# Rounding turns in the matmul accumulator: one TensorE step for one VectorE step, a norm moved to ScalarE, and new instruction orders

## The chip, the cores and the metric

The kernel runs on one NeuronCore of a Trainium2 chip. Five engines work side by side: TensorE (PE in the profile, with its weight loads as PEld), VectorE (DVE), ScalarE (ACT), GpSimd (POOL) and SyncE (SP), which here only issues DMAs. Each takes its own instructions in a fixed order and waits at the head of its queue for what the instruction needs. The metric is the device time of one execution in microseconds (us), lower is better.

## The reference

Four layers are applied to a 2048x512 array, each after a layer norm and with a residual: a two-dimensional Fourier filter (A), a long convolution along the rows (B), then A and B once more with the same parameters.

```
def _A_ref(x, w_r, w_i):
    X = rfft2(x) * (w_r + 1j * w_i)
    return irfft2(X)
def _B_ref(u, log_A_real, A_imag, C_real, C_imag, log_dt, D_skip):
    dt = exp(log_dt); A = -exp(log_A_real) + 1j * A_imag
    P = exp((A * dt[:, None])[:, :, None] * arange(L))         # D x N x L
    K = 2 * einsum("dn,dnl->dl", (C_real + 1j * C_imag) * dt[:, None], P).real
    return irfft(rfft(u_t, 2L) * rfft(K, 2L))[:L] + u * D_skip
x = x + _A_ref(_layernorm(x));  x = x + _B_ref(_layernorm(x))
x = x + _A_ref(_layernorm(x));  x = x + _B_ref(_layernorm(x))
```

K, the kernel of the convolution, needs the cosine and sine of a phase for every channel, state and position. Its sum over 128 states for 512 channels and 2048 positions is a large part of the work, and both B layers use the one K.

## The kernel before

All transforms are matmuls with constant tables. Almost every matmul is issued in two halves of 64 output rows (`halves`, lines 325 to 330), so that the two column halves of the array work at once: this is the tile shape 128x64. The rows transform of a B layer (`rows` in `forward_b`, through `side_by_side`, lines 333 to 336) has 64 rows of contraction and uses the shape 64x64, four products at once. A change from one shape to the other is called a change of tile shape below.

The program has these stages: the start (loads, first layer norm, the small vectors that K is made of, `kernel_parts`), the first layer A (`layer_a`), the first layer B (`forward_norm`, `forward_b`, `layer_b`), the second layer A, the second layer B. Making K (`kernel_time`) runs beside the first two layers, because it needs nothing from them; its frequency form (`kernel_freq`) is needed block by block by the first layer B.

`kernel_time` works through 32 units. For each, `grow` makes three magnitudes by Exp on ScalarE, one of them by a product on GpSimd. `bend` then makes phases for each of two halves of a unit, 64 times in all. A phase is counted in turns (whole circles), so only its fraction matters. Two pairs of bf16 matmuls put the turns into a PSUM tile `pk` of 512 columns, 256 each (`KQ`, `KP`); VectorE adds and subtracts 1.5x2^23, which rounds to a whole number, and writes it as bf16 into the SBUF tile `kw` (line 864); a third pair of matmuls with minus the identity (`ni`) subtracts it from the turns in PSUM. On ScalarE `sine` takes the absolute value and the sine, `cosine` takes the sine with a quarter turn added. `terms` on VectorE (lines 886 and 888) multiplies them with the magnitudes, `total` sums over states on TensorE into `pv` (line 899), and ScalarE copies that out (line 907). The `pk` tiles rotate over three PSUM banks.

In the first layer B, `forward_norm` loads four row groups of the normed array by a DMA into a tile `w`, and applies the layer norm with a scale and a bias per partition from `norms`. `XNE` names the engine of each of the four: 'gggg' is GpSimd (line 1113), 64 instructions of 128x128 in all. These tiles are the weights' side of the 64x64 matmuls.

The order of the work on every engine is written out. `take_turns` numbers an engine's instructions as the code makes them and chains them in the order of the table `TURNS`; no instruction passes another on its engine. `ROOMS` says which buffer of a rotating tag each new tile takes. `WARM` (used in `ps`, line 312) puts throwaway matmuls on the tile `warm` ahead of the first use of some PSUM tiles: each count is one pair of halves, which keeps TensorE's activity up.

## Time and profile before

| | before |
|---|---|
| times of three runs | 716.46 us median (710.45, 716.46, 718.14) |
| span of the profiled execution, first to last instruction | 713.4 us |
| busy: TensorE, VectorE, ScalarE, GpSimd | 626.0, 601.9, 438.2, 357.3 us |
| mean granted TensorE clock, share of full speed | 0.973 |
| rows of matmuls on `warm` | 924 of 9580, 73.8 us busy |
| ACT table loads | 24 |

The profiled execution's own time is shown only as its span; the median of the runs is 3.1 us above that span. A matmul's row in the profile lasts from its start to its modelled end, which lies after the time at which the next one can start, so rows of TensorE overlap and its busy time is more than the time for which it is taken. A float32 matmul makes two rows, a bf16 one makes one.

### The profile page before, as it was taken

How to read it: one execution, taken by the hardware profiler on the slowest of the kernel's cores; microseconds unless marked ns; L12 is line 12 of the kernel's file. 1: busy time of each engine (PE TensorE's matmuls, PEld its weight loads, DVE VectorE, ACT ScalarE, POOL GpSimd, SP SyncE). 2: the span in 40 equal slices, each digit the busy share in tenths (PEclk: the TensorE clock that was granted, in tenths of full speed). 3: DMA queues.
4: the chain of work that ended last, by engine and by line, in shares of the span. 5: the costliest groups of instructions: out<-in, count | busy, mean ns of one | idle time of the engine just before them, and what ended most of it. 6: DMA issues, size and time to landing. Idle time of an engine off the chain costs nothing. (4 is left out here: it accounts for less than half of the span.)

```text
span 713.4 us, 23503 instructions
## 1 busy us (share of the span) xinstructions
PE 626.0 (88%) x9580; PEld 491.3 (69%) x9580; DVE 601.9 (84%) x1348; ACT 438.2 (61%) x946; POOL 357.3 (50%) x565
## 2 busy tenths in 40 slices
PE   4459989989996999889999997984989899999996
PEld 3237867878674867667858876774877766577876
DVE  4998497998999799969999676869588699799993
ACT  3558999997664796778868524333767427333322
POOL 1533528672852704543196356452056484286870
PEclk9779999999999999999999999997999999999999
DMA  8602611613558350455544689222123103335514
GB/s 282 229 0 89 210 48 47 122 62 43 167 133 245 107 138 32 65 128 94 163 62 136 195 198 246 80 106 75 61 77 89 46 2 104 125 103 149 156 34 111
DMA packets 137355, 81.32 MB, mean 114 GB/s; under 512 B 70976, under 2 KB 116928, under 8 KB 136352
## 3 DMA queue, kind: packets, MB, share of 16 engines
q1 hardware_dynamic: 136992, 79.30, 40.1%
q8 instruction: 76, 1.25, 0.7%
q0 software_dynamic: 256, 0.52, 0.4%
q14 instruction: 31, 0.25, 0.1%
HBM read 54.90 MB, written 25.43 MB: 113 GB/s over the span
## 5 line engine op out<-in xcount | busy, mean ns | idle before, releaser
L1003 POOL TENSOR_TENSOR u<-wb,wb 64x512 f32<-64x512 f32 x90 | 123.2, 1373 | 66.0 <-DVE wb L991 60.9
L336 PE MATMUL p<-z,mb 128*64 128x512 f32 (+2 forms) x480 | 108.0, 517 | 1.7 <-DVE wb L991 1.3
L899 PE MATMUL pv<-qp 128*64 128x128 f32 x1024 | 81.6, 279 | 5.0 <-ACT stage L907 4.2
L991 DVE TENSOR_TENSOR wb<-p,kk 128x512 f32<-128x512 f32 x128 | 81.5, 676 | 4.3 <-POOL u L1003 2.3
L336 PEld LDWEIGHTS p<-mb,u 128*64 128x64 f32 x2048 | 73.1, 138 | 13.1 <-issue 6.7
L336 PE MATMUL p<-mb,u 128*64 128x64 f32 x2048 | 74.3, 223 | 4.4 <-issue 2.0
L663 ACT COPY z<-p 128x512 f32<-128x512 f32 x96 | 52.4, 595 | 41.8 <-PE p L336 31.6
L669 DVE STREAM_TRANSPOSE z<-z 128x512 f32<-128x512 f32 x96 | 59.3, 675 | 19.8 <-ACT z L663 19.7
L899 PEld LDWEIGHTS pv<-qp 128*64 128x64 f32 x1024 | 64.4, 139 | 15.8 <-ACT stage L907 6.9
L1113 POOL TENSOR_SCALAR w<-w,norms 128x128 f32<-128x128 f32 x64 | 34.7, 554 | 67.7 <-DMA w<-h 29.8
L547 POOL TENSOR_TENSOR w<-w,w 64x257 f32<-64x257 f32 x48 | 34.7, 724 | 66.8 <-DVE w L542 45.3
L1015 ACT COPY u<-p 128x512 f32<-128x512 f32 x64 | 35.9, 590 | 48.7 <-PE p L336 45.3
L330 PE MATMUL p<-w,w 128*64 128x256 f32 x256 | 38.2, 438 | 27.8 <-DVE w L463 11.6
L330 PE MATMUL pk<-kb,th 96*64 96x256 bf16 (+1 forms) x384 | 56.5, 312 | 1.5 <-DVE qp L888 1.1
L542 DVE TENSOR_TENSOR w<-wt,p 128x514 f32<-128x514 f32 x64 | 42.7, 688 | 17.1 <-PE p L336 9.6
L864 DVE TENSOR_SCALAR kw<-pk 128x512 bf16<-128x512 f32 x64 | 42.9, 680 | 16.5 <-PE pk L330 16.1
L330 PE MATMUL p<-warm 128*64 128x128 f32 x612 | 49.2, 284 | 3.2 <-DVE half L1139 1.1
L336 PE MATMUL p<-t,w 64*64 64x128 f32 x1024 | 42.1, 280 | 10.2 <-DMA w<-kt 3.5
L336 PEld LDWEIGHTS p<-z,mb 128*64 128x64 f32 x480 | 39.7, 137 | 16.1 <-issue 7.9
L330 PEld LDWEIGHTS p<-w,w 128*64 128x64 f32 x256 | 24.7, 156 | 36.3 <-DVE w L463 12.7
L336 PE MATMUL p<-w,ca 128*64 128x257 f32 x256 | 45.0, 385 | 4.1 <-ACT w L526 1.5
L832 ACT ACTIVATE kf<-pk 128x512 f32<-128x512 f32 x64 | 38.8, 606 | 15.4 <-PE pk L330 13.8
(179 smaller groups left out, 1617.1 us busy)
## 6 DMA issues: line engine op xcount, KB each, us to landing
wt<-in_w SPq DMA_DIRECT2D x32, 257.0 KB, 2.7
kf<-kk SPq DMA_DIRECT2D x32, 256.0 KB, 3.3
kk<-kf SPq DMA_DIRECT2D x32, 256.0 KB, 2.7
u<-in_x SPq DMA_DIRECT2D x16, 256.0 KB, 6.8
hr<-in_x SPq DMA_DIRECT2D x16, 256.0 KB, 3.9
kt<-stage SPq DMA_DIRECT2D x32, 128.0 KB, 5.2
h<-hr SPq DMA_DIRECT2D x16, 256.0 KB, 3.0
w<-kt SPq DMA_DIRECT2D x32, 128.0 KB, 3.1
```

Of the source, the lines that this page charges most:

```text
L330: self.nc.tensor.matmul(out[64 * r:64 * r + 64], weights[:, 64 * r:64 * r + 64], data, **k)
L336: last = self.nc.tensor.matmul(out, weights, data, start=not more, stop=True, skip_group_check=True).ins
L542: nc.vector.tensor_mul(m[pl], W, px[:, None, :].to_broadcast([128, 2, 257]))
L547: e[0].tensor_sub(Y[0:64, v], m[0][hs, 0], m[1][hs, 1])
L663: nc.scalar.copy(tiles["z"][:, :, :, b, m:m + 2].rearrange("p u j m r -> p (u j) (m r)"), ps[b].rearrange("p u j m r -> p (u j) (m r)"))
L669: nc.vector.transpose(tiles["zt"][:, u:u + 8].rearrange("p u j d -> p (u j d)"), tiles["z"][:, u:u + 8].rearrange("p u j b m r -> p (u j b ...
L832: nc.scalar.activation(*a, **k)
L864: nc.vector.tensor_scalar(whole, p, MAGIC, -MAGIC, op0=ALU.add, op1=ALU.add)
L899: nc.tensor.matmul(p[64 * t:64 * t + 64, g], QP[:, c, 2, d:d + 2].rearrange("p s a -> p (s a)"), QP[:, c, 0:2, d:d + 2].rearrange("p k s b ...
L991: nc.vector.tensor_mul(split(m[c, pl], "du", [32, 16]), by_channel(p), split(k[c], "du", [32, 16]))
L1003: self.added = e[0].tensor_sub(y[0:64], v[0, 0], v[1, 1]), e[1].tensor_add(y[64:128], v[0, 1], v[1, 0])
L1015: nc.scalar.copy(V[:, :, j, :, d:d + 8].rearrange("p n q d -> p q n d"), p.rearrange("p (q n) d -> p q n d", q=2))
```

## The change

Five things change.

1. `bend` no longer uses VectorE. After the two pairs of products, two more pairs of matmuls add 1.5x2^23 to the PSUM tile and subtract it again: weights `ni`, now a row of ones or of minus ones in the first of 128 partitions, and a new tile `big` that holds the constant. The accumulation in PSUM rounds. Two last pairs with negated tables (`LQ`, `LP`) subtract the turns, so the tile holds the whole number minus the turns, and the sine's scale changes its sign. The tile `kw` is gone; `kb`, `ni` and the new `big` take more SBUF than before.
2. `XNE` is 'aaaa': the 64 norm instructions go to ScalarE, as an Identity with scale and bias.
3. `phase` makes every buffer of a pool once at its start, in the order of the call, and two calls list their tags in another order.
4. `TURNS` and `ROOMS` are new for all engines and pools.
5. `WARM` goes from 231 pairs in 92 places to 12 pairs in two.

```
-XNE = 'gggg'
+XNE = 'aaaa'
...
-    out["ni"] = -np.eye(128)
-    out["kb"] = kb.reshape(96, 2560)
+    first = np.zeros((128, 2, 128))
+    first[0, 0], first[0, 1] = 1, -1
+    out["ni"] = first.reshape(128, 256)
+    out["kb"] = np.concatenate([kb, -kb[:, :, :512], -kb[:, :, 1536:2048]], 2).reshape(96, 3584)
...
+            for tag, v in tags.items():
+                if not isinstance(v, str):
+                    for k in range(v[1]):
+                        room = f"{tag}{k}" if v[1] > 1 else tag
+                        pool.tile([128, v[0] // 4], F32, tag=room, bufs=1, name=f"{name}_{room}")
...
+        self.big = self.sb("big", [512], dt=BF)
+        self.nc.gpsimd.memset(self.big, MAGIC)
...
-            whole = self.sb("kw", [512], dt=BF)
             p = self.ps("pk", [2, 256])
-            self.halves(p[:, 0], th[:, h, 0], KQ[:, e], start=True, stop=False, skip_group_check=True)
-            self.halves(p[:, 1], th[:, h, 1], KP[:, e], start=False, stop=False, skip_group_check=True)
+            a, b = th[:, h, 0], th[:, h, 1]
+            self.halves(p[:, 0], a, KQ[:, e], start=True, stop=False)
+            self.halves(p[:, 1], b, KP[:, e], start=False, stop=False)
+            p0, p1 = p[:, 0], p[:, 1]
             p = p.rearrange("p k d -> p (k d)")
-            nc.vector.tensor_scalar(whole, p, MAGIC, -MAGIC, op0=ALU.add, op1=ALU.add)
-            self.halves(p, self.ni, whole, start=False, stop=True, skip_group_check=True)
+            self.halves(p, self.ni[:, 0:128], self.big, start=False, stop=False)
+            self.halves(p, self.ni[:, 128:256], self.big, start=False, stop=False)
+            self.halves(p0, a, LQ[:, e], start=False, stop=False)
+            self.halves(p1, b, LP[:, e], start=False, stop=True)
...
-            ordered(p, p, ACT.Sin, scale=-TAU)
+            ordered(p, p, ACT.Sin, scale=TAU)
...
-WARM = {22: 7, 35: 3, 55: 1, 104: 3, 116: 2, 120: 5, 123: 6, 146: 2, 158: 1, 160: 2,
+WARM = {39: 5, 1184: 7}
```

Lines 330, 336, 832, 899 and 1113 of the kernel before are lines 337, 343, 841, 911 and 1123 of the changed one.

The first place is TensorE amid the making of K. Before, a bend's last product (`pk_278`) is followed by the subtraction of two earlier bends, whose rounded numbers `kw` came from VectorE, and by a sum `pv`:

```order
L330 LDWEIGHTS th_231_1298
L330 MATMUL pk_278_1505<-kb_9_88,th_231_1298 64x256
L330 LDWEIGHTS ni_10_89
L330 MATMUL pk_261_1425<-kw_260_1424,ni_10_89 64x512
L330 LDWEIGHTS ni_10_89
L330 MATMUL pk_261_1425<-kw_260_1424,ni_10_89 64x512
L899 MATMUL pv_236_1312<-qp_203_1123 64x128 x8
L330 LDWEIGHTS ni_10_89
L330 MATMUL pk_274_1487<-kw_273_1486,ni_10_89 64x512
L330 LDWEIGHTS ni_10_89
L330 MATMUL pk_274_1487<-kw_273_1486,ni_10_89 64x512
L330 MATMUL p1_228_1263<-ca_126_745,w_212_1169 64x128 x2
```

In the changed program a bend's products, the two steps of the constant and the subtraction of the turns stand behind each other (`pk_253` here, from its fourth product on):

```order
L337 LDWEIGHTS th_224_1300
L337 MATMUL pk_253_1422<-kb_9_117,th_224_1300 64x256
L337 LDWEIGHTS ni_10_118
L337 MATMUL pk_253_1422<-big_11_119,ni_10_118 64x512
L337 LDWEIGHTS ni_10_118
L337 MATMUL pk_253_1422<-big_11_119,ni_10_118 64x512
L337 LDWEIGHTS ni_10_118
L337 MATMUL pk_253_1422<-big_11_119,ni_10_118 64x512
L337 LDWEIGHTS ni_10_118
L337 MATMUL pk_253_1422<-big_11_119,ni_10_118 64x512
L337 LDWEIGHTS th_224_1300
L337 MATMUL pk_253_1422<-kb_9_117,th_224_1300 64x256
```

What moved: nothing of a bend waits for VectorE any more, and a bend has twelve matmuls where it had six.

The second place is the first norm of the first layer B. Before, it stands on GpSimd, between the last folds of layer A (`wv`) and the magnitudes of K (`mag`):

```order
L604 COPY wv_589_2970<-w_588_2967 128x4
L1113 TENSOR_SCALAR w_672_3405<-w_672_3405,norms_419_2219 128x128 x4
L1113 TENSOR_SCALAR w_676_3443<-w_676_3443,norms_419_2219 128x128 x4
L847 TENSOR_TENSOR e32_691_3572<-mag_689_3561 128x16
L848 TENSOR_TENSOR mag_689_3561<-mag_689_3561,e32_691_3572 128x512
```

In the changed program it stands on ScalarE, between the sines of K (`qp`, `kf`, `pk`) and copies out of PSUM (`z`):

```order
L841 ACTIVATE kf_705_3784<-pk_698_3742 128x512
L1123 ACTIVATE w_641_3436<-w_641_3436,norms_399_2257 128x128
L841 ACTIVATE pk_689_3702<-pk_689_3702 128x512
L841 ACTIVATE pk_698_3742<-pk_698_3742 128x512
L841 ACTIVATE qp_704_3783<-kf_705_3784,half_3_67 128x512
L670 COPY z_601_3202<-p1_603_3206 128x128x4
L670 COPY z_601_3202<-p1_608_3235 128x128x4
L1123 ACTIVATE w_645_3472<-w_645_3472,norms_399_2257 128x128 x2
L1123 ACTIVATE w_641_3436<-w_641_3436,norms_399_2257 128x128
```

What moved: a norm that has to wait for its row DMA or for `norms` now holds up the sines of K behind it, and no longer the magnitudes on GpSimd.

The third place is the head of SP's queue, the first loads. Before, five rows of x (`u`) and a part of the table `ta` go ahead of the vectors for K (`raw`):

```order
L428 DMA u_7_83<-in_x 128x512 x5
L322 DMA ta_18_118<-in_ta 128x512
L739 DMA raw_39_247<-in_kin 128x2048
L428 DMA u_7_83<-in_x 128x512
L740 DMA raw_39_247<-in_log_dt 128x4
```

In the changed program `raw` goes first:

```order
L746 DMA raw_40_274<-in_kin 128x2048
L435 DMA u_7_107<-in_x 128x512 x6
L329 DMA ta_19_155<-in_ta 128x512
L435 DMA u_7_107<-in_x 128x512
L747 DMA raw_40_274<-in_log_dt 128x4
```

What moved: the 1 MB of `raw` passes five rows of x and a part of `ta`.

More of the change, by code (lines that the diff above doesn't have):

```diff
@@ L809, in kernel_constants @@
         BF = mybir.dt.bfloat16
-        self.kb = self.sb("kb", [2560], dt=BF, rows=96)
-        self.ni = self.sb("ni", [128], dt=BF)
+        self.kb = self.sb("kb", [3584], dt=BF, rows=96)
+        self.ni = self.sb("ni", [256], dt=BF)
+        self.big = self.sb("big", [512], dt=BF)
+        self.nc.gpsimd.memset(self.big, MAGIC)
         self.nc.gpsimd.dma_start(self.kb, self.cst["kb"])
@@ L821, in kernel_time @@
         KB = self.kb
-        KQ, RM, RN, KP, RP = (KB[:, k:k + 512] for k in range(0, 2560, 512))
+        KQ, RM, RN, KP, RP, LQ, LP = (KB[:, k:k + 512] for k in range(0, 3584, 512))
         state = {}
@@ L1147, in net_kernel @@
             with net.phase("p", P, p1=(2048, 8 - PK - PV), p2="p1", p3="p1"), \
-                    net.phase("a", x=(32768, 1), ta=(8192, 1), ca=(6912, 1), u=(16384, 2), w=(2056, WA), wt=(2056, WT),
+                    net.phase("a", x=(32768, 1), u=(16384, 2), ta=(8192, 1), w=(2056, WA), ca=(6912, 1), wt=(2056, WT),
                               wv="w", junk="w"):
                 A = net.layer_a(w, src=xv, dst=hd)
-                early.enter_context(net.phase("k0", side="right", kb=(5120, 1), ni=(256, 1), th=(1536, TH)))
+                early.enter_context(net.phase("k0", side="right", kb=(7168, 1), ni=(512, 1), big=(1024, 1), th=(1536, TH)))
                 net.kernel_constants()
@@ L1158, in net_kernel @@
                     net.end_weights(ends)
-                    early.enter_context(net.phase("k", side="right", kw=(1024, 2), mag=(6144, MAG),
+                    early.enter_context(net.phase("k", side="right", mag=(6144, MAG),
                                                   qp=(6144, QP), kf=(2048, KF), stage=(8192, 1)))
@@ L1169, in net_kernel @@
             outer.enter_context(net.phase("f", t=(16384, 1), z=(16384, 2), w=(2056, WB)))
-            outer.enter_context(net.phase("b", t2=(8192, 1), u=(16384, 2), kk=(2048, 8), ta="t2", wt="w", wb="w", xw="w"))
+            outer.enter_context(net.phase("b", kk=(2048, 8), t2=(8192, 1), u=(16384, 2), ta="t2", wt="w", wb="w", xw="w"))
             pm = [int(c) for c in PM.split(",")]
@@ L1494 @@
     "folds.xf": "0101",
-    "pc.p1": "0101010101010101010101010101010101010101010110010101011001011001",
-    "pc.p2": "2102102102102102102102102102102102102102102102102102102102102102",
+    "pc.p1": "0101001101100110010010100101010101011001010110101001011001101010",
+    "pc.p2": "0201121021202102120121101201122012012012100202101012012002120120",
 }
```

468 lines of the change are left out of this document (226 added, 242 removed), and 9 rows, old and new, of the table WARM.

## The prediction

> **What bounds the kernel now.** I read the page's busy line first, then the table of busy time by stretches, then the waits. The busy line:
>
> ```profile
> PE 626.0 (88%) x9580; PEld 491.3 (69%) x9580; DVE 601.9 (84%) x1348; ACT 438.2 (61%) x946; POOL 357.3 (50%) x565
> ```
>
> TensorE looks like the bound, VectorE second. The stretch in which the change works is given by the rounding's rows (the view of the tile `kw`, first and last start at the end of the numbers), and the next view splits the span around it:
>
> ```profile
> L864 DVE TENSOR_SCALAR kw<-pk x64: 650/681/693, 79.8 to 382.9; 128x512 bf16<-128x512 f32 x64
> ...
> core 0: us, PE busy (x) PEld busy (x) DVE busy (x) ACT busy (x) POOL busy (x), PEclk, DMA share, GB/s
> 0.00:54.00 54.00, 24.92 (x169) 16.87 (x171) 43.65 (x117) 25.74 (x53) 19.38 (x39) 0.81 0.51 169
> 54.00:396.00 342.00, 317.02 (x4660) 249.89 (x4657) 306.85 (x676) 273.64 (x564) 174.58 (x304) 0.99 0.42 109
> 396.00:486.00 90.00, 80.04 (x1422) 64.97 (x1418) 64.83 (x145) 34.01 (x65) 48.83 (x55) 1.00 0.62 168
> 486.00:713.00 227.00, 204.06 (x3336) 159.53 (x3336) 186.56 (x413) 104.77 (x266) 114.48 (x167) 0.97 0.29 87
> ```
>
> I call 54 to 396 us the K stretch. The same table for rows that touch `warm` alone (TensorE first):
>
> ```profile
> 54.00:396.00 342.00, 49.12 (x620) 37.28 (x620) 0.00 (x0) 0.99 0.42 109
> 396.00:486.00 90.00, 8.92 (x124) 8.07 (x124) 0.00 (x0) 1.00 0.62 168
> 486.00:713.00 227.00, 10.64 (x136) 7.88 (x136) 0.00 (x0) 0.97 0.29 87
> ```
>
> Without `warm`, TensorE's rows in the K stretch are 317.0 - 49.1 = 267.9 us of 342 (78%), VectorE's are 306.9 (90%), ScalarE's 273.6 (80%). VectorE is the bound there. Its waits in that stretch, and TensorE's for it (total, times, longest):
>
> ```profile
> DVE kw L864 <- PE pk L330: 16.1, 8, 7.5
> DVE z L669 <- ACT z L663: 4.4, 2, 4.0
> PE pk L330 <- DVE kw L864: 2.2, 4, 0.8
> ```
>
> VectorE is idle 342 - 306.9 = 35.1 us, and 16.1 of it stands ahead of the rounding. One more thing is needed before TensorE's side is priced. In the timeline, a bf16 pair of 512 columns lasts 0.39 us, but the next row starts 0.22 us after it:
>
> ```profile
> 184.40 0.39 PE L330 MATMUL pk<-kb,th 96*64 96x512 bf16 x2
> 184.62 1.48 PE L330 MATMUL p<-ca,u 128*64 128x256 f32 x20
> ```
>
> I call 0.22 us its slot; a pair of 256 columns is put at half, 0.11 us.
>
> **The change part by part.**
>
> *Rounding.* The rows that go and that come (busy us and mean ns behind the bar):
>
> ```profile
> L864 DVE TENSOR_SCALAR kw<-pk 128x512 bf16<-128x512 f32 x64 | 42.9, 680 | 16.5 <-PE pk L330 16.1 <-PE p L336 0.2
> ...
> L330 PE MATMUL pk<-kb,th 96*64 96x256 bf16 x256 | 31.1, 274 | 0.6 <-DVE qp L888 0.5
> L330 PE MATMUL pk<-kw,ni 128*64 128x512 bf16 x128 | 29.3, 382 | 2.4 <-DVE kw L864 2.2
> L330 PE MATMUL pk<-kb,th 96*64 96x512 bf16 x128 | 25.7, 387 | 1.0 <-DVE qp L888 0.6 <-ACT mag L832 0.3
> ```
>
> VectorE loses 42.9 us of work and the 16.1 us of wait. TensorE gains, per bend, two pairs of 256 columns and, net, one pair of 512 (two with the constant come, one with `kw` goes): 2 x 0.11 + 0.22 = 0.44 us, x 64 = 28.2 us by slots. By shown rows it is 31.1 more for the 256-column group, and 128 pairs at 25.7 / 64 = 0.40 us less 29.3 for the others, together +53 us. I take the slots, because in the crowded stretches one row starts a slot behind the other; 53 is kept as the upper bound. All of it stands on the path if TensorE becomes the bound. The setting of `big`, one instruction on GpSimd ahead of the first bend, costs nothing while GpSimd waits for work in the start (19.4 busy of 54 us).
>
> *Norm.* GpSimd loses 64 rows; ScalarE gets them. No row is just this instruction there. The nearest is one of the same size with a scale per partition alone (397 ns), the far one has scale and bias and four times the columns (808 ns):
>
> ```profile
> L1113 POOL TENSOR_SCALAR w<-w,norms 128x128 f32<-128x128 f32 x64 | 34.7, 554 | 67.7 <-DMA w<-h 29.8 <-DVE norms L382 19.4 <-PE p L336 12.5
> ...
> L458 ACT ACTIVATE w<-ta,lnn 128x128 f32<-128x128 f32 x16 | 6.3, 397 | 1.0 <-DVE lnn L378 0.6 <-PE p L330 0.3
> ...
> L627 ACT ACTIVATE x<-za,lnn 128x512 f32<-128x512 f32 x16 | 12.1, 808 | 1.7 <-DVE lnn L382 1.6
> ```
>
> I take 0.45 us: 64 x 0.45 = 29 us, bounds 25 and 52. 44 of them lie in the K stretch (the table of stretches for rows that touch `norms`, VectorE and GpSimd):
>
> ```profile
> 54.00:396.00 342.00, 1.79 (x12) 26.02 (x44) 0.99 0.42 109
> ```
>
> If these stay there, ScalarE has 273.6 + 20 = 293 us of work in it (86%). Beside TensorE that is hidden; if TensorE had room it would be last. On GpSimd 34.7 us go, from an engine that was half idle: worth nothing by itself.
>
> *Changes of tile shape.* Counted along TensorE's order, there are 92 before and 154 after; of the 62 more, 38 stand in the part of the order up to the last sum of K. A run of 64x64 work between two others in the timeline, and two rows of one column half, 128 float32 columns each:
>
> ```profile
> 143.77 0.27 PE L899 MATMUL pv<-qp 128*64 128x128 f32 x1
> ...
> 143.88 0.27 PE L899 MATMUL pv<-qp 128*64 128x128 f32 x1
> ...
> 646.37 1.10 PE L336 MATMUL p<-t,x 64*64 64x128 f32 x32
> 647.41 2.84 PE L336 MATMUL p<-u,t 128*64 128x128 f32 x48
> 650.18 1.10 PE L336 MATMUL p<-t,x 64*64 64x128 f32 x32
> ```
>
> The slot of 128 columns is 0.11 us. The first run has 32 rows in eight groups of four, 0.88 us, and takes 1.04; the next has 24 pairs, 2.64 us, and takes 2.77. So a change costs about 0.15 us (0.13 to 0.16): 38 x 0.15 = +5.7 us in the K stretch, 24 x 0.15 = +3.6 us behind it. If the 0.15 us were a wait for data at these two places and not the change itself, the term would be nothing and the sum 5.7 us less. The Trainium skill ("TensorEngine Tiling (Array Packing)", Key Properties) decides for the first: changing the tiling mode, not just the tile, drains the TensorE, so every one of the 62 pays, and by it the sum is the one below, without it 691. The trace agrees in that both of the quoted changes pay the same.
>
> *Throwaway matmuls.* 219 of 231 pairs go. A pair has two float32 rows per half, so 0.22 us: 48 us of slots. They stand ahead of a tile's first product, mostly in TensorE's waits; behind the K stretch 65 pairs (260 rows) are 14 us, of which I let a third be in the way: -4.8 us. In the K stretch I count them as wholly hidden, since TensorE has 342 - 267.9 = 74 us without work there.
>
> *Start.* VectorE's first waits, from the timeline:
>
> ```profile
> 3.54 0.69 DVE L359 BATCH_NORM_STATS2 bst<-u 128x6 f32<-128x512 f32 x1 [2.46 <-DMA u<-in_x]
> ...
> 10.13 1.29 DVE L359 BATCH_NORM_STATS2 bst<-u 128x6 f32<-128x512 f32 x2 [5.67 <-DMA u<-in_x]
> ...
> 16.01 0.43 DVE L696 TENSOR_SCALAR raw<-raw 128x516 f32<-128x516 f32 x1 [1.01 <-DMA raw<-in_log_dt]
> ```
>
> With `raw` ahead of x, the wait of 5.67 can be filled with K's vectors, but the first row of x comes later: between -6 and +6 us (its 1 MB at the 169 GB/s of the row 0 to 54 us would be 6 us). I take -1.
>
> *Orders and buffers* behind the K stretch have no row that prices them: the same work in another order, 0 with 8 us either way. With -4.8 and +3.6 I put that part at -1, and nothing on the new buffers of `phase`.
>
> **The sum**, for the K stretch. VectorE: 306.9 - 42.9 + 35.1 - 16.1 = 283 us. TensorE: 267.9 + 28.2 + 5.7 + its other waits as today (342 - 317.0 - 2.2 = 22.8) = 324.6 us. TensorE is late next, and the stretch goes from 342 to 324.6: -17.4. With the start (-1) and the rest (-1) that is -19.4 on a span of 713.4, so 694.0. The median of the runs lies 3.1 above the span, which gives 697.
>
> **The rivals.**
>
> *More is gained.* TensorE's own rows overlap, so it is less full than 267.9 says, and waits shrink where no round trip is left. Then ScalarE is last. Its densest part is this (fourth of the busy times):
>
> ```profile
> 54.00:108.00 54.00, 50.78 (x638) 42.44 (x635) 42.24 (x86) 50.47 (x111) 21.29 (x55) 1.00 0.36 115
> ```
>
> 293 us at that share, 50.47 of 54 or 0.935, is 314, so -28. With -5 for the throwaway pairs and -1: 716.5 - 34 = 682. For it: 16.1 us of VectorE's wait and its 90%. Against it: 0.44 us more per bend on TensorE.
>
> *TensorE is full already.* By its shown rows: 267.9 + 53 + 5.7 + 22.8 = 349, +7; with half of that and -2 elsewhere 718, no change.
>
> *Slower: ScalarE held up by norms.* This is the longest wait that moves (total, times, longest):
>
> ```profile
> POOL w L1113 <- DMA w<-h: 29.8, 6, 14.7
> POOL w L1113 <- DVE norms L382: 19.4, 2, 16.0
> ```
>
> On GpSimd they delay little; on ScalarE the sines of K are queued behind, and TensorE's sums behind those. If the 29.8 us for the DMA come whole onto the path, 697 + 30 = 727. It decides from some 19 us on, where the gain is used up. Against it: the new order can put a norm later than its data.
>
> *Clock.* The granted clock falls behind a stretch in which TensorE does little (its busy time, then the clock):
>
> ```profile
> 227.10:230.52 3.42, 1.03 (x23) 1.00 1.02 326
> 230.52:233.93 3.41, 3.41 (x48) 0.50 0.98 271
> ```
>
> 3.41 us at half speed lose at most 1.7 us. If a dozen more such stretches come where the throwaway pairs stood, that is +20: 717. The Trainium skill ("TensorE: Matmul & The Clock Gate", Why this matters for your kernels) says it so: no idle gaps over about 3 us between bursts, else half rate. The trace agrees that one such stretch is enough. I give it little, since the real work grows where the pairs go.
>
> **How the numbers follow.** Chances: forecast 0.45 (686 to 708), more gained 0.22 (672 to 690), TensorE full 0.16, norms 0.12, clock 0.05. The predicted time is 697. For eight in ten I go from 672, the far end of more gained, to 726, which leaves out most of the norm case and the ends. About 1% (7 us) is what a measurement of this kernel can tell from no change. Faster by over 1% (under 709.3): nearly all of the first, and the second, 0.65. Within 1%: most of TensorE full and of the clock case, 0.19. Slower: the norms and the ends of the others, 0.16.
>
> **What would show it.** No rows of VectorE on `pk` but `terms`; its busy time near 559. On TensorE 128 pairs on `big` with slots of 0.22 us, its busy time without `warm` up by 28 to 53 us. The last sum of K (`pv`) some 18 us earlier than its last start at 412.5 us here, if the first terms hold:
>
> ```profile
> L899 PE MATMUL pv<-qp x1024: 270/273/475, 90.9 to 412.5; 128*64 128x128 f32 x171
> ```
>
>  ScalarE's 64 norms near 0.45 us, and its waits for `w<-h`: more than 19 us would speak for the slower rival. The page's row of the granted clock, where three slices of 40 stand at 7 tenths now; five more would speak for the clock:
>
> ```profile
> PEclk9779999999999999999999999997999999999999
> ```
>
>  I am wrong at the root if VectorE is still at 85% or more in the K stretch, or if TensorE's waits grow by what VectorE lost.

## The result, and the profile after

The changed kernel takes 710.41 us (median of 20 runs, 706.91 to 712.63) against 717.65 us for the kernel before (20 runs beside them): ratio 0.9911, 95% interval 0.9894 to 0.9929. That is 0.9% faster; 2.7% was forecast (697 us). The span of the profiled execution went from 713.4 to 710.0 us.

The changed kernel's busy line, and its table of busy time by stretches (K stretch second; behind the clock stand DMA share and GB/s):

```profile
PE 638.6 (90%) x9088; PEld 471.8 (66%) x9088; DVE 569.6 (80%) x1284; ACT 459.5 (65%) x1009; POOL 325.4 (46%) x502
...
core 0: us, PE busy (x) PEld busy (x) DVE busy (x) ACT busy (x) POOL busy (x), PEclk, DMA share, GB/s
0.00:54.00 54.00, 23.69 (x182) 14.02 (x184) 44.61 (x125) 26.96 (x63) 20.35 (x44) 1.00 0.48 163
54.00:396.00 342.00, 331.55 (x4636) 251.07 (x4633) 280.15 (x629) 297.53 (x621) 150.78 (x256) 1.00 0.47 119
396.00:486.00 90.00, 74.22 (x1182) 55.16 (x1182) 70.28 (x177) 38.43 (x91) 39.57 (x36) 0.94 0.54 150
486.00:710.00 224.00, 209.13 (x3096) 151.55 (x3092) 174.54 (x355) 96.57 (x238) 114.65 (x166) 0.96 0.28 83
```

TensorE is now busy for 97% of the K stretch, VectorE for 82% (90% before), ScalarE for 87%. Three rows of the view by tiles (min, median, max of one in ns; first and last start in us): the last K sum of the changed kernel, and the first matmul on `pk` of the kernel before and of the changed one.

```profile
L911 PE MATMUL pv<-qp x1024: 270/273/324, 82.5 to 390.1; 128*64 128x128 f32 x171
```

```profile
L330 PE MATMUL pk<-kb,th x384: 269/274/634, 70.7 to 379.8; 96*64 96x256 bf16 x128, 96*64 96x512 bf16 x64
```

```profile
L337 PE MATMUL pk<-kb,th x640: 269/273/403, 64.8 to 365.5; 96*64 96x256 bf16 x129, 96*64 96x512 bf16 x31
```

The last K sum starts at 390.1 us instead of 412.5: 22.4 us earlier, 5.9 of them already there at the first matmul on `pk`. From there to the end the kernel before takes 713.4 - 412.5 = 300.9 us and the changed one 710.0 - 390.1 = 319.9. So 19 us are given back behind the last K sum. Two rows by tiles tell where, of the kernel before and of the changed one: the last normed row of the second layer A (`x<-za,lnn`) and the last forward sum of the second layer B (`p<-t,x`).

```profile
L627 ACT ACTIVATE x<-za,lnn x16: 799/804/825, 590.2 to 609.0; 128x512 f32<-128x512 f32 x16
...
L336 PE MATMUL p<-t,x x512: 269/269/320, 595.5 to 674.3; 64*64 64x128 f32 x171
```

```profile
L634 ACT ACTIVATE x<-za,lnn x16: 798/810/825, 576.7 to 593.2; 128x512 f32<-128x512 f32 x16
...
L343 PE MATMUL p<-t,x x512: 269/269/473, 579.1 to 669.9; 64*64 64x128 f32 x171
```

The lead of 22.4 us is 15.8 at the end of the second layer A (593.2 against 609.0), 4.4 at the last forward sum of the second layer B (669.9 against 674.3) and 3.4 at the end. Some 7 us go between the last K sum and the second layer A's end, and 11.4 in the forward part of the second layer B.

That last stretch, in the table of busy time, in the kernel before and in the changed one:

```profile
609.00:674.30 65.30, 63.25 (x1206) 47.19 (x1202) 59.56 (x95) 23.14 (x46) 45.23 (x34) 1.00 0.40 120
```

```profile
593.20:669.90 76.70, 75.49 (x1168) 46.35 (x1166) 58.77 (x94) 23.46 (x47) 45.40 (x34) 0.94 0.30 96
```

The same work, without the throwaway pairs, takes 76.7 instead of 65.3 us, at a mean clock of 0.94. The norms and the bends are as foreseen (rows by tiles, and ScalarE's wait ahead of the norms: total, times, longest):

```profile
L1123 ACT ACTIVATE w<-w,norms x64: 477/494/536, 227.6 to 417.2; 128x128 f32<-128x128 f32 x64
L337 PE MATMUL pk<-big,ni x256: 377/379/411, 71.1 to 362.7; 128*64 128x512 bf16 x128
...
ACT w L1123 <- DMA w<-h: 2.2, 3, 1.2
```

A norm takes 0.494 us on ScalarE, and the norms together wait 2.2 us for `h`, not 29.8: the forecast's slower rival did not come.

### The profile page after: what moved, and what is told of

The parts are those of the page before. It is cut to its first block, busy times and chain, and to the rows that moved or that the text cites. A ratio compares the mean times of both kernels' runs of the same rounds, so it can differ in the third digit from the quotient of the medians.

```text
span 710.0 us, 22381 instructions
## 1 busy us (share of the span) xinstructions
PE 638.6 (90%) x9088; PEld 471.8 (66%) x9088; DVE 569.6 (80%) x1284; ACT 459.5 (65%) x1009; POOL 325.4 (46%) x502
## 5 line engine op out<-in xcount | busy, mean ns | idle before, releaser
L343 PE MATMUL p<-z,mb 128*64 128x512 f32 (+2 forms) x480 | 138.6, 523 | 3.1 <-ACT kk L966 1.7
L911 PE MATMUL pv<-qp 128*64 128x128 f32 x1024 | 102.5, 276 | 1.0 <-DVE qp L900 0.5
L337 PE MATMUL pk<-kb,th 96*64 96x256 bf16 (+1 forms) x640 | 92.4, 296 | 1.9 <-ACT mag L841 1.1
L911 PEld LDWEIGHTS pv<-qp 128*64 128x64 f32 x1024 | 75.0, 136 | 17.7 <-issue 7.6
L676 DVE STREAM_TRANSPOSE z<-z 128x512 f32<-128x512 f32 x96 | 59.9, 679 | 12.5 <-ACT z L670 11.6
L337 PEld LDWEIGHTS <-th 96*64 96x64 bf16 x640 | 49.1, 109 | 23.9 <-issue 14.0
L1027 ACT COPY u<-p 128x512 f32<-128x512 f32 x64 | 37.1, 587 | 42.9 <-PE p L343 42.7
L343 PEld LDWEIGHTS p<-z,mb 128*64 128x64 f32 x480 | 43.3, 137 | 31.3 <-issue 16.1
L337 PE MATMUL p<-ca,u 128*64 128x128 f32 (+2 forms) x512 | 59.3, 312 | 1.3 <-ACT u L570 1.2
L337 PEld LDWEIGHTS p<-ca,u 128*64 128x64 f32 x512 | 45.0, 142 | 13.5 <-issue 6.2
L337 PE MATMUL pk<-big,ni 128*64 128x512 bf16 x256 | 52.6, 381 | 0.0
L343 PEld LDWEIGHTS p<-t,w 64*64 64x64 f32 x1024 | 34.3, 137 | 26.7 <-issue 15.1
L856 POOL TENSOR_TENSOR e<-mag 128x16 f32<-128x16 f32 x32 | 9.4, 299 | 89.7 <-DVE z L676 44.3
```

Of the source, the lines that this page charges most:

```text
L337: self.nc.tensor.matmul(out[64 * r:64 * r + 64], weights[:, 64 * r:64 * r + 64], data, **k)
L343: last = self.nc.tensor.matmul(out, weights, data, start=not more, stop=True, skip_group_check=True).ins
L676: nc.vector.transpose(tiles["zt"][:, u:u + 8].rearrange("p u j d -> p (u j d)"), tiles["z"][:, u:u + 8].rearrange("p u j b m r -> p (u j b ...
L856: e.tensor_mul(t, m[:, :, 31], m[:, :, 1])
L911: nc.tensor.matmul(p[64 * t:64 * t + 64, g], QP[:, c, 2, d:d + 2].rearrange("p s a -> p (s a)"), QP[:, c, 0:2, d:d + 2].rearrange("p k s b ...
L1027: nc.scalar.copy(V[:, :, j, :, d:d + 8].rearrange("p n q d -> p q n d"), p.rearrange("p (q n) d -> p q n d", q=2))
```

## The experiments

All ratios are to the kernel before, run beside each kernel (its medians there lay between 716.3 and 718.6 us), with the 95% interval.

| kernel | median us | ratio |
|---|---|---|
| rounding alone, old orders | 743.5 | 1.0372 (1.0337 to 1.0407) |
| the same, no pairs in the K stretch | 736.2 | 1.0250 (1.0207 to 1.0293) |
| the same with pairs, new matmuls early | 732.0 | 1.0211 (1.0159 to 1.0263) |
| before without VectorE's rounding | 718.7 | 1.0006 (0.9973 to 1.0040) |
| before, no pairs in the K stretch | 709.3 | 0.9878 (0.9849 to 0.9907) |
| before, new order in the start | 726.7 | 1.0127 (1.0092 to 1.0162) |
| before, new tail | 728.6 | 1.0155 (1.0094 to 1.0217) |
| changed, old tail | 697.2 | 0.9745 (0.9717 to 0.9774) |
| changed, old tail without its pairs | 700.6 | 0.9782 (0.9754 to 0.9810) |
| changed, pairs in the tail's waits | 711.8 | 0.9925 (0.9901 to 0.9949) |
| changed, norms on GpSimd | 706.4 | 0.9859 (0.9806 to 0.9913) |
| changed, old tail, norms on GpSimd | 694.6 | 0.9673 (0.9633 to 0.9713) |
| the same, old order from about 425 us | 706.3 | 0.9842 (0.9801 to 0.9883) |
| changed, no rounding at all | 711.2 | 0.9913 (0.9884 to 0.9942) |
| changed, K stretch's pairs put back | 734.6 | 1.0243 (1.0189 to 1.0297) |
| changed, VectorE loaded | 723.0 | 1.0059 (1.0027 to 1.0092) |
| changed, ScalarE loaded | 726.4 | 1.0101 (1.0044 to 1.0159) |

### The rounding alone, in the old orders

```diff
 # kernel before; TURNS, ROOMS, WARM and XNE stay
-            nc.vector.tensor_scalar(whole, p, MAGIC, -MAGIC, op0=ALU.add, op1=ALU.add)
-            self.halves(p, self.ni, whole, start=False, stop=True, skip_group_check=True)
+            self.halves(p, self.ni[:, 0:128], self.big, start=False, stop=False)
+            self.halves(p, self.ni[:, 128:256], self.big, start=False, stop=False)
+            self.halves(p0, th[:, h, 0], LQ[:, e], start=False, stop=False)
+            self.halves(p1, th[:, h, 1], LP[:, e], start=False, stop=True)
```

> The kernel before with one part of the change alone: the rounding in PSUM by TensorE. Norms stay on GpSimd, and the order of every engine, the rooms and all 231 throwaway pairs stay those of before (the eight new matmuls of a bend stand where its two `kw` matmuls stood). Theory 1, the prediction's sum for the K stretch holds and everything behind it was lost to the new orders: the last sum of K comes 15 to 20 us earlier, what lies behind takes its 301 us as before, and the time is 698 to 703 us, faster than the whole change (710.4). Theory 2, the rounding alone gives little, since the old order has TensorE wait or work where it did, and the 22 us in the K stretch came from the new order: 709 to 717 us.

Measured: 743.5 us, 27 us slower than before, which neither theory had. The K stretch in the table of busy time, the last K sum by tiles, and two of the waits:

```profile
54.00:396.00 342.00, 316.45 (x4482) 254.05 (x4480) 252.72 (x573) 257.58 (x529) 156.66 (x287) 0.98 0.40 101
...
L907 PE MATMUL pv<-qp x1024: 270/273/473, 92.3 to 438.2; 128*64 128x128 f32 x171
...
DVE qp L894 <- ACT pk L837: 26.3, 21, 4.4
ACT kf L837 <- PE pk L332: 21.5, 21, 3.3
```

VectorE's busy time in 342 us falls from 306.9 to 252.7, and the work ends 25.7 us later (438.2 against 412.5). VectorE now waits 26.3 us for ScalarE's sines (3.4 us in the kernel before, in the same view) and these 21.5 us for TensorE (13.8 before). In the old orders a part of what VectorE was freed of turned into waiting.

### VectorE's rounding taken away, nothing put in its place

```diff
 # kernel before; `big` is set to zero
-            nc.vector.tensor_scalar(whole, p, MAGIC, -MAGIC, op0=ALU.add, op1=ALU.add)
-            self.halves(p, self.ni, whole, start=False, stop=True, skip_group_check=True)
+            self.halves(p, self.ni[:, 0:128], self.big, start=False, stop=True)
```

> The kernel before, its orders and all its throwaway pairs, without VectorE's rounding: the 64 rows on `kw` (42.9 us) are left out, and the two matmuls of a bend that read `kw` read a constant zero instead, so TensorE's work stays the same and waits for nothing (the sines are then taken of arguments that are not reduced). Theory 1, the prediction's reading that VectorE sets the pace of the K stretch: 43 us of work and 16 us of wait less give 686 to 702 us. Theory 2, in this order VectorE's rows lie beside TensorE's: 709 to 718 us, and the rounding alone lost its 27 us because nothing stood against the 28 us of slots.

Measured: 718.7 us, no change. Its busy line, its K stretch and its last K sum:

```profile
PE 626.5 (88%) x9580; PEld 495.3 (69%) x9580; DVE 570.9 (80%) x1284; ACT 438.2 (61%) x946; POOL 356.8 (50%) x566
...
54.00:396.00 342.00, 315.39 (x4620) 250.03 (x4618) 275.09 (x611) 273.66 (x565) 173.11 (x304) 0.98 0.43 109
...
L903 PE MATMUL pv<-qp x1024: 270/273/473, 91.8 to 414.8; 128*64 128x128 f32 x171
```

VectorE is at 80% in the K stretch instead of 90% and has no wait for `pk` any more; the last K sum still starts at 414.8. Its wait for ScalarE's sines went from 3.4 to 20.4 us. So VectorE did not set the pace of the kernel before in its order, although it was its fullest engine there. The run also prices the new matmuls: rounding alone and this kernel differ in six matmuls a bend, 743.5 - 718.7 = 24.8 us or 0.39 us a bend, where the forecast had 0.44. That price goes for the place at which the old order has them; a run below moves them and takes 11.5 us off it.

### The throwaway pairs of the K stretch, and the place of the new matmuls

```diff
 # kernel before: WARM without the 155 pairs of the K stretch
-WARM = {22: 7, 35: 3, 55: 1, 104: 3, ... 1035: 1, 1105: 7, ...}
+WARM = {22: 7, 35: 3, 55: 1, 1105: 7, ...}
```

> The kernel before without the 155 throwaway pairs that stand in the K stretch (33 us of slots); rounding, norms, orders and the 76 other pairs stay. Theory 1, the prediction's: VectorE sets the pace there and the pairs only fill TensorE's waits: 714 to 722 us, no gain, some more half clock. Theory 2, TensorE's row of work is what sets the pace in the K stretch, pairs included: 685 to 705 us, and the change's 22 us in that stretch are those of the pairs that it leaves out.

> The rounding alone in the old orders (743.5 us) without the same 155 pairs. Theory 1, the pairs are hidden: 738 to 746 us, and it is the new order that pays for the rounding in the changed kernel. Theory 2, TensorE sets the pace: the pairs' 33 us of slots and the rounding's 28 us weigh about the same, 708 to 722 us, that is, the change's gain in the K stretch is from the pairs and not from VectorE's 43 us.

Measured: 709.3 us for before without them, which is as much as the whole change brought; 736.2 us for the rounding alone without them. The first lies between the two theories: of 33 us of slots 8 come back. In the order in which the rounding alone is slow they bring 7. In TensorE's rows of the kernel before up to the last K sum the rest went into waits (gaps between the starts of rows, longer than the slot by over 0.3 us: 34 us before, 61 without pairs) and into rows at half clock. So in the old order leaving out the pairs brings 8 us and not the K stretch's whole gain, and the rounding costs its 27 us with them and without. What the pairs weigh in the new order is measured below, and it is more.

```diff
 # rounding alone, order of TensorE: each bend's eight new matmuls right behind its first four
-  KQ KQ KP KP  (some 20 other matmuls)  big x4 LQ LQ LP LP
+  KQ KQ KP KP big x4 LQ LQ LP LP  (some 20 other matmuls)
```

> The rounding alone in the old orders, with the eight new matmuls of a bend put right behind its first four (in the old order some 20 matmuls lie between, which once covered VectorE's round trip). Theory 1, the place costs: sines start some 20 matmuls earlier and the time falls from 743.5 to 712 to 728 us. Theory 2, the slots cost wherever they stand: 738 to 748 us.

Measured: 732.0 us, between the theories. 11.5 of the 27 us are the place: the old order keeps a distance for a round trip that no longer exists. Against the kernel without any rounding on VectorE (718.7) the new matmuls now cost 13.3 us, or 0.21 us a bend.

### The changed kernel with the old tail, and the kernel before with the new one

```diff
 # changed kernel, from the first quarter of the second layer A on (about 496 us)
-TURNS, ROOMS, WARM of the changed kernel
+TURNS, ROOMS, WARM of the kernel before (34 throwaway pairs)
```

> The changed kernel up to the first quarter of the second layer A (about 496 us), and from there on the order of every engine, the rooms and the 27 throwaway pairs of the kernel before; the work is the same. Theory 1, order, rooms and throwaway pairs of the tail gave back some 11 us in the second layer B: 697 to 701 us. Theory 2, the loss is not in the tail's order but comes from what the K stretch leaves behind: 708 to 712 us.

> As the kernel with the tail of before, but without its 27 throwaway pairs: old order and rooms from about 496 us on, no throwaway matmul there. Theory 1a, the order itself (shape changes of TensorE's tile, rows of one column half behind each other) cost the 11 us: as fast as with the pairs, 697 to 702 us. Theory 1b, the missing pairs and with them the half clock cost them: 704 to 711 us, with new stretches at half clock between 496 and 680 us.

Measured: 697.2 us with the pairs (34 by the table, not 27) and 700.6 without. The old tail gives back 13.2 us, 9.8 of it by its order and rooms alone and 3.4 by its pairs (the intervals of these two kernels overlap, so the 3.4 are near the noise), though apart from the pairs both kernels have the same instructions there. The second layer B of the kernel with the old tail, from the last normed row to the last `p<-t,x` (busy table, and by tiles):

```profile
593.00:657.00 64.00, 63.10 (x1208) 47.27 (x1204) 59.18 (x95) 23.17 (x46) 45.13 (x34) 1.00 0.41 124
...
L343 PE MATMUL p<-t,x x512: 269/269/320, 579.6 to 657.0; 64*64 64x128 f32 x171
```

64.0 us, as in the kernel before (65.3), against 76.7 in the changed one. What the new order does there is seen in TensorE's timeline of the changed kernel:

```profile
602.13 1.96 PE L343 MATMUL p<-z,mb 128*64 128x32 f32 x6
604.02 0.43 PE L343 MATMUL p<-t,x 64*64 64x128 f32 x4
604.38 1.08 PE L343 MATMUL p<-z,mb 128*64 128x512 f32 x4
605.39 0.70 PE L343 MATMUL p<-t,x 64*64 64x128 f32 x8
606.03 1.08 PE L343 MATMUL p<-z,mb 128*64 128x512 f32 x4
```

The old order has runs of 32 rows of `p<-t,x` between sums on `z` (the prediction's row at 646.37 us is one: 32 rows in 1.10 us); here they stand in fours and eights. From the starts of TensorE's rows, the time of this stretch comes apart so (us; slots as in the prediction):

| 2nd layer B, last `x` to last `p<-t,x` | before | changed | changed, old tail |
|---|---|---|---|
| slots of the real rows | 51.3 | 51.0 | 51.3 |
| slots of throwaway pairs | 1.7 | 0 | 1.7 |
| beyond the slot at changes of tile shape (count) | 5.3 (27) | 9.4 (40) | 5.3 (27) |
| beyond the slot, same shape, under 0.3 us a row | 3.9 | 9.2 | 3.9 |
| gaps over 0.3 us | 3.3 | 6.9 | 1.9 |
| sum | 65.5 | 76.5 | 64.1 |

Of the 11 us a good third stands at changes of tile shape, waits at these places included, the rest in short waits between rows and in gaps. A change is not dearer by itself: half of them take at most 0.17 us in both kernels, but 16 of 40 take about 0.3 us or more in the changed kernel and 6 of 27 before. 6.7 us of what the changed kernel has beyond its slots lies in the stretch at half clock.

```diff
 # kernel before, from the same point on
-TURNS, ROOMS, WARM of the kernel before
+TURNS, ROOMS, WARM of the changed kernel
```

> The kernel before up to the first quarter of the second layer A, and from there on the order, rooms and (no) throwaway pairs of the changed kernel: the mirror of the kernel with the old tail. Theory 1, the new tail by itself costs its 13 us wherever it follows: 727 to 733 us. Theory 2, it costs only behind the new K stretch: 714 to 722 us.

Measured: 728.6 us, 11 us slower than before. The loss belongs to the tail's order, rooms and missing pairs together, and it comes behind either K stretch.

### The clock

```diff
 # changed kernel: pairs ahead of the tiles first used at 421, 469, 545, 547, 592 and 596 us
-WARM = {39: 5, 1184: 7}
+WARM = {39: 5, 1087: 8, 1184: 22, 1380: 3, 1381: 3, 1527: 6, 1547: 5}
```

> The changed kernel with 40 throwaway pairs more, in the waits that stand ahead of four of its five stretches at half clock behind the K stretch (ahead of the tiles that are first used at 421, 469, 545, 547, 592 and 596 us), nothing else moved. Theory 1, the granted clock took most of what was given back behind the K stretch (27 us of half clock, some 13 us lost): most of these stretches go, and the time falls by 7 to 12 us to 699 to 703. Theory 2, the clock matters little there and the new order is what costs: within 2 us of 710.4, or up to 4 us longer for the pairs that now stand in the way.

Measured: 711.8 us against 710.4: no gain. The pairs do what they are for. One of the places in the table of busy time, in the changed kernel and in the one with pairs:

```profile
540.80:544.20 3.40, 2.87 (x30) 1.87 (x26) 3.00 (x7) 1.46 (x6) 1.86 (x4) 1.00 0.31 80
544.20:547.60 3.40, 1.77 (x24) 1.29 (x26) 2.55 (x6) 1.27 (x4) 1.91 (x3) 1.00 0.00 0
547.60:554.40 6.80, 6.06 (x46) 5.01 (x45) 0.75 (x2) 1.02 (x3) 1.07 (x3) 0.50 0.01 2
```

```profile
544.20:547.60 3.40, 2.70 (x44) 2.34 (x42) 3.29 (x7) 0.65 (x2) 2.25 (x4) 1.00 0.00 0
547.60:554.40 6.80, 5.31 (x81) 4.62 (x77) 1.40 (x4) 1.68 (x6) 1.32 (x4) 1.00 0.01 2
```

The mean granted clock goes from 0.979 to 0.995, and three of four stretches at half clock between 420 and 603 us are gone. The profiled span is 2.5 us shorter (707.5), 1.9 of them in the second layer B (592.6 to 667.4, 74.8 us for 76.7); the medians do not show it. So of the 13 us that 27 us at half clock seem to lose, nearly nothing came back. The run tells only the net of the clock and of 40 pairs (8.8 us of slots by the prediction's 0.22 us): what the clock costs without them is not shown.

### What sets the pace of the K stretch in the new order

```diff
 # changed kernel: rounding left out
-            self.halves(p, self.ni[:, 0:128], self.big, start=False, stop=False)
-            self.halves(p, self.ni[:, 128:256], self.big, start=False, stop=False)
-            self.halves(p0, a, LQ[:, e], start=False, stop=False)
-            self.halves(p1, b, LP[:, e], start=False, stop=True)
```

> The changed kernel without any rounding: the eight matmuls of a bend on `big`, LQ and LP are left out, so that the sines are taken of arguments that are not reduced (what they do to the output is of no interest here). Takes 64 x 0.66 us = 42 us of slots from TensorE in the K stretch and nothing from another engine. Theory 1, TensorE sets the pace there in the changed kernel too: 672 to 688 us. Theory 2, ScalarE (87% busy there) or VectorE (82%) is late next at once: 695 to 706 us.

Measured: 711.2 us, nothing gained. 324 us of the K stretch in the busy table, changed kernel and this one, and this one's last K sum:

```profile
54.00:378.00 324.00, 313.55 (x4350) 238.29 (x4347) 271.31 (x602) 283.69 (x588) 150.78 (x256) 1.00 0.46 116
```

```profile
54.00:378.00 324.00, 287.65 (x3820) 208.12 (x3816) 268.46 (x599) 280.71 (x584) 150.84 (x256) 0.97 0.46 116
...
L907 PE MATMUL pv<-qp x1024: 270/273/475, 81.9 to 391.8; 128*64 128x128 f32 x171
```

TensorE was 97% busy, 42 us of slots go, and the last K sum starts at 391.8 instead of 390.1. Up to there 41 us of slots went; 31 us came back as gaps over 0.3 us (15 to 47) and some 11 us at rows in half clock and at changes of tile shape. Both theories fail: TensorE's rounding work does not set the pace, and ScalarE and VectorE, at 87 and 83%, are not full either.

```diff
 # changed kernel; GpSimd's order with the norms where ScalarE had them among the others' work
-XNE = 'aaaa'
+XNE = 'gggg'
```

> The changed kernel with the 64 norms back on GpSimd, each at the place in GpSimd's order that it has among the other engines' work in the changed kernel; nothing else moved. Theory 1, the norms are beside the path on either engine: 708 to 713 us. Theory 2, ScalarE's 29 us of norms hold up the K stretch: 700 to 707. Theory 3, GpSimd's share in the new order is needed: 714 to 722 us.

Measured: 706.4 us, at most 4 us better (its interval and the change's overlap). The last K sum is at 389.5 us: 16 us less on ScalarE in the K stretch (281.2 us busy instead of 297.5) move it by 0.6.

```diff
 # changed kernel: the 155 pairs of the K stretch put back, ahead of the first matmul of their tiles
-WARM = {39: 5, 1184: 7}
+WARM = {39: 5, 105: 3, 117: 2, 121: 5, 124: 6, ... 974: 1, 1184: 7}
```

> The changed kernel with the 155 throwaway pairs of the K stretch put back, each ahead of the first matmul of its tile, 33 us of slots. Theory 1, TensorE has room in the new order (42 us of slots taken away brought nothing there): 707 to 716 us. Theory 2, TensorE is full in the new order (97% busy by its rows) and the run without rounding hid that behind half clock: 728 to 745 us, and the pairs that were left out are then a large part of the K stretch's gain.

```diff
 # changed kernel, one of the two a kernel, at the head of a bend's sines
+            nc.vector.tensor_scalar(self.kw, self.even0, MAGIC, -MAGIC, op0=ALU.add, op1=ALU.add)
+            nc.scalar.copy(self.kw, self.even0)
```

> The changed kernel with one more instruction on VectorE per bend: a rounding of 480 constant float32 columns into a tile that nobody reads, ahead of the bend's first product, 64 x about 0.6 us = 38 us, nearly what `kw` took before. Theory 1, VectorE has room in the new order (82% busy in the K stretch): 710 to 718 us. Theory 2, VectorE is what sets the pace there now (taking 42 us from TensorE and 11 from ScalarE brought nothing): 735 to 750 us.

> The same on ScalarE: a copy of 480 constant columns per bend, ahead of its first sine, 64 x about 0.55 us = 35 us. Theory 1, ScalarE has room (87% busy in the K stretch, some 44 us of 342 idle): 710 to 720 us. Theory 2, every engine of the new order is at its end: 735 to 748 us, as with the throwaway pairs put back on TensorE.

Measured: pairs back 734.6 us, VectorE loaded 723.0, ScalarE loaded 726.4. Last K sums, and the rows of the added work (busy us, mean ns), of the three kernels:

```profile
L911 PE MATMUL pv<-qp x1024: 270/273/324, 86.0 to 417.2; 128*64 128x128 f32 x171
```

```profile
L915 PE MATMUL pv<-qp x1024: 270/273/324, 83.3 to 406.0; 128*64 128x128 f32 x171
...
L885 DVE TENSOR_SCALAR kw<-dum 128x480 bf16<-128x480 f32 x64 | 35.5, 555 | 0.1
```

```profile
L915 PE MATMUL pv<-qp x1024: 270/273/324, 82.8 to 406.1; 128*64 128x128 f32 x171
...
L885 ACT CAST kw<-dum 128x480 bf16<-128x480 f32 x64 | 39.1, 612 | 0.1
```

Loads of 33, 35.5 and 39.1 us cost 24, 12.5 and 16 us, and the last K sum comes 27, 16 and 16 us later. With the pairs back the second theory holds: the last K sum is then at 417.2 us, later than the 412.5 of the kernel before, so in the new order the whole gain of the K stretch hangs on leaving the pairs out. The two other runs lie between their theories. Each of the three engines costs part of what is put on it, and taking from TensorE or from ScalarE returned next to nothing; taking from VectorE was not tried. This fits a chain from TensorE to ScalarE to VectorE and back in which each has little slack and none alone sets the pace, but that picture is argued and not shown.

### The start, and a better kernel

```diff
 # kernel before: first part (up to about 60 us) in the order and rooms of the changed kernel
-TURNS, ROOMS of the kernel before
+TURNS, ROOMS of the changed kernel
```

> The kernel before with the new order and rooms in its first part alone (K's vectors, `raw` ahead of x; up to about 60 us), all else as before. Theory 1, the start's 6 us (first matmul on `pk` at 64.8 us against 70.7) come from the order of the start and are kept to the end: 709 to 713 us. Theory 2, the old order behind it is not ready for them, and they are given back in the K stretch: 715 to 719 us.

Measured: 726.7 us, slower than both theories. The first matmul on `pk` comes at 66.9 us (70.7 before), but the first K sum only at 101.1 (90.9 before): at the seam of the two orders K's last vectors (`hp`) are put off from 73.9 to 85.6 us. The run is inconclusive on the start itself.

```diff
 # changed kernel with the old tail (697.2 us)
-XNE = 'aaaa'
+XNE = 'gggg'
```

> The kernel with the tail of before (697.2 us) and the norms on GpSimd as in the run of that alone (706.4 against 710.4 us). Theory 1, the two add up: 691 to 696 us. Theory 2, the norms' 4 us were no more than the spread of the runs: 696 to 699 us.

```diff
 # the same, but the old order, rooms and pairs begin in the last block of the first layer B (about 425 us)
```

> As the kernel with the tail of before and norms on GpSimd, but the old order, rooms and pairs begin earlier, in the last block of the first layer B (about 425 us). Theory 1, the 7 us that the new order lost between the last sum of K and the second layer A come back as well: 684 to 691 us. Theory 2, they come from what the K stretch leaves undone (layer B's work that the K sums then no longer cover), or the seam between the two orders costs as much: 692 to 700 us.

Measured: 694.6 us, 3.3% faster than before and the best of all; 706.3 us with the earlier seam. The 7 us between the last K sum and the second layer A's end did not come back that way, and whether the seam or the K stretch is to blame was not separated.

## Why the prediction was wrong, point by point

**The failed step is the last term of its sum**, "0 with 8 us either way. With -4.8 and +3.6 I put that part at -1": behind the K stretch the change lost 19 us in the profile. 13.2 of them come back with the old tail, and the new tail costs 11 on the kernel before. The same instructions in another order and other rooms were worth 9.8 us, more than the forecast's bound of 8 and more than the whole change. With the old tail the kernel takes 697.2 us, the forecast's number, but not by the forecast's terms: that is luck, as the next paragraphs show. In the profile of that kernel 5.3 of the 19 us remain behind the last K sum (its span of 695.5 less 389.3 us, against 300.9 before); their cause stays open.

- *Throwaway pairs behind K.* The term took -4.8 us for leaving them out. In the old tail, leaving out its 34 pairs costs 3.4 us, near the noise: no gain is seen, and the sign was probably wrong.
- *Changes of tile shape.* 0.15 us each was close. Over all of them up to the last K sum the next row starts late by 13.1 us at 51 changes before and by 16.8 us at 80 changes after; that is 0.26 and 0.21 us each, but with waits of up to 2.7 us in it. Half of them take at most 0.17 us in both kernels, and 46 of 51 and 65 of 80 take 0.15 to 0.20. The place was off: by the rows of the traces 29 of the 62 more lie up to the last K sum, not 38, and 33 behind it. The Trainium skill ("TensorEngine Tiling (Array Packing)", Key Properties) says that a change of mode drains TensorE and gives no time. The traces agree in that the next row starts late at every change, by 0.15 us or more up to the last K sum.

**The K stretch came out at the forecast size by luck, for another reason.** The last K sum is 22.4 us earlier. 5.9 stand at the first matmul on `pk` already (the start was put at -1 within -6 to +6), and 16.5 come after it, where -17.4 was forecast. But "VectorE is the bound there" was wrong for the order that the kernel had. Taking VectorE's 42.9 us and its 16.1 us of waits away brought nothing (718.7 us), and moving the rounding to TensorE without the new order cost 27. From the starts of TensorE's rows, the way from 54 us to the last K sum (358.6 us before, 336.1 after) has 33.1 us less of slots of throwaway pairs and 19.0 less of gaps over 0.3 us (34.4 to 15.4), against 18.2 more of slots of real rows, 3.7 more at changes of tile shape and 7.6 more of short waits. The largest term, the pairs, is one that the prediction put at nothing; its own main terms, VectorE's work and its waits, were not what held the old order up. The account by medians of runs (us, each from the kernel in the line above):

| step | us |
|---|---|
| before without the K stretch's pairs (717.7 to 709.3) | -8 |
| rounding by TensorE, old orders (to 736.2) | +27 |
| new order and rooms up to about 496 us, norms on ScalarE, 12 pairs for 42 there (to 697.2) | -39 |
| new order and rooms behind it, without pairs (to 710.4) | +13 |

So the step with the new order before 496 us is what pays, and it pays for the rounding too: in the new order the rounding costs nothing (711.2 without it). It does not pay by itself. With the K stretch's pairs put back the changed kernel loses 24 us, with a load like the old rounding put back on VectorE 12.5, so the steps do not simply add up, and their sizes go for this sequence alone. Some 11.5 us of the 39 may be the place of the new matmuls, which was measured in the old order, and part the start; what the rest is made of stays open. The new order with the rounding still on VectorE was not run, so how much of the gain needs the rounding on TensorE at all is not shown.

- *Price of a bend.* 0.44 us on TensorE by slots; measured 0.39 in the old order, 0.21 with the new matmuls moved forward there, and nothing in the new order. The slots came out as an upper bound of what a bend costs here, and the bound by shown rows (+53) was not needed. TensorE's busy time without `warm` rose by 83 us (626.0 - 73.8 to 638.6 - 3.2), far above the 28 to 53 that the prediction named as its sign: shown rows overlap and are no measure of time used.
- *"Throwaway matmuls wholly hidden" in the K stretch.* Leaving them out brought 8 of 33 us in the old order; putting them back in the new one cost 24.
- *Norm.* 0.45 us forecast, 0.494 measured; 2.2 us of waits against the 19 from which the slower rival decided. On ScalarE they cost at most 2.6 to 4 us (697.2 against 694.6, 710.4 against 706.4).
- *TensorE full already.* The rival's 718 rested on the price of the bends, and in the new order these cost nothing. TensorE has little room there all the same, as the 24 us for the pairs show.
- *Clock.* Behind the last K sum 27 us run at half clock instead of 10, apart from the last 4 us of the span, but over the whole span it is less than before (the mean clock is 0.979 against 0.973). The rival's sign, five more slices at 7 tenths, did not come; with most of these stretches taken away the time stayed.
- *The sign for being wrong at the root* was VectorE at 85% or more in the K stretch. It fell to 82%, and the reading was wrong all the same. The other sign, TensorE's waits growing, did not come either (gaps 34.4 to 15.4 us). VectorE's busy time is 569.6 us, 11 above the 559 named. A busy share under or over a bound does not say who sets the pace; a run without the work does, for the order in which it is made.

## What to carry to other kernels

The fullest engine of a stretch is not its bound until its work has been taken away and the time has followed: in the old order 59 us of VectorE's work and waits were worth nothing, while 0.39 of 0.44 us a bend on TensorE was paid. Such a price goes for one order: in the new one the bends' matmuls are free, and a load of 35.5 us on VectorE costs 12.5. When a change brings a new order with it, price the order as a term of its own, stage by stage, by running the old order behind the new one; the stages can then be mixed, and here the mix (694.6 us) beats both kernels. Look at a moved computation's place as well: an order made for a round trip keeps its distance when the round trip is gone.

## What was not expected of the hardware

- The clock halves without a long pause of TensorE. The 3.4 us ahead of the stretch at 547.6 us hold 1.77 us of rows (quoted above) and no gap over 0.79 us in the timeline; in the stretch that the prediction quotes, 227.10 to 230.52 us of the kernel before, the longest gap is 2.39 us. Against drops of the clock in mid-kernel the Trainium skill ("TensorE: Matmul & The Clock Gate", Why this matters for your kernels) asks that no idle gap between bursts is over some 3 us. The trace does not agree that this is enough.
- Taking half clock away by throwaway matmuls returned nothing: with 40 pairs more and a mean clock of 0.995 instead of 0.979 the median is 711.8 against 710.4 us.
- In the new order load and relief are not symmetric: 33 us put on TensorE cost 24, 42 us taken from it returned nothing.
